# VectorE copies that free a PSUM bank get the rank of score tiles, with new planner settings

## The chip, the cores and the metric

The kernel runs on one core of a Trainium2 chip. The core has five engines with a queue of instructions each: TensorE (PE), ScalarE (ACT), VectorE (DVE), GpSimd (POOL) and SyncE (SP, which here only issues DMAs). Matmuls write into PSUM, which has eight banks of 512 fp32 values on each of 128 partitions. The metric is the time of one execution on the device, in microseconds; lower is better. The time before is the median of three runs.

## The reference

The input x has 2048 rows of 512 features. Two layers of attention and gated FFN are applied, each with a residual and a layer norm ahead:

```python
x = x + A(layernorm(x), wqkv, wo)                 # 32 heads of width 16, softmax over all 2048 keys
x = x + B(layernorm(x), w_gate, w_up, w_down)     # (gelu(x @ w_gate) * (x @ w_up)) @ w_down, width 1792
x = x + A(layernorm(x), wqkv, wo)                 # the same weights again
x = x + B(layernorm(x), w_gate, w_up, w_down)
```

Attention without a mask means 32 heads x 2048 x 2048 scores in each layer, every one of which goes through an exponential.

## The kernel before, in words

**Units and tiles.** A unit is one block of 512 queries and four heads; there are 32 units a layer (the last eight of layer two are cut in halves of 256 queries). A unit has 64 score tiles of 128 keys x 512 queries, each of which fills one PSUM bank. TensorE computes up to four tiles at a time, one for each quarter of its rows (L1555). ScalarE takes the tiles of a "slot" together, three banks or two in turn, and writes exp of them to `PT` in bf16 (L1569).

**Tiles on VectorE.** Up to about a third of the tiles may go to VectorE instead. It takes no exponential: it adds a bias, clips at zero and converts to int16 (L1609, into `PI`), so that the bits read as fp16 are roughly a power of two. Up to four such tiles make a group. For each group, three further instructions (L1649, "half-steps" in this text: `PP` = `PI` plus a constant) make the same numbers shifted by a quarter, a half and three quarters of a power, and the sum of four products with rescaled values (`VP` and three copies `VD`) smooths the error out. TensorE multiplies all of it with the values (P·V, L1701), accumulating in bank 7. When a unit is done, VectorE copies bank 7 out (L1001, L996).

**Banks.** Banks 0 to 2 and 3 to 4 are ScalarE's two slots, bank 7 the accumulator. Banks 5 and 6 float: every other product goes through them, that is, VectorE's score tiles and all "pieces" of side work. A piece is a few matmuls into one bank: Q, K and V projections (L654, L731), output projection (L654 to L1208), gate and up (L1223), down (L1287). Behind a piece, VectorE copies the bank out (L702, L721, L752, L1208, L1242 for gate, L1266 for up, L1318 and L1309 for down), and only then is the bank free again. `evac_job` (L578) is the helper that queues this copy.

**The order is written by a planner.** The Python code simulates the engines while it emits instructions: each has a modelled cost, and `sch.ready` tells when its inputs are there in the model. The main loop (L1851) follows TensorE's time and picks, in this order: the next fill of a slot when its banks are free; a batch of P·V; a piece of side work from one of five sources; a smaller batch of P·V; or filler (`keep_clock`, L1715, matmuls of zeros[...]) when the share of streaming time in the last 3.4 us is below `DENSE`.

**The job queues.** VectorE, GpSimd and SyncE get their work through `jobs` (L472). `pump_one` (L495) looks at all queued jobs of an engine, finds the earliest that could start, and among those within 0.03 us of it takes the one of the lowest rank, then the oldest. Score copies (L1609) have rank 0, as has the copy of bank 7; half-steps and most bank-freeing copies rank 1; layer norm statistics 1 or 2. [...]

**When VectorE gets a tile.** `pick` (L1428) looks through the tiles in order for one that VectorE may take, if a floating bank is free within 0.02 us and `vector_tile` (L1406) is true: VectorE's queue, its running work, the queued jobs and 0.37 us for each half-step that waits for a buffer, must come to less than `DVE_LATE`. `fill_ready` (L1469) may hold a fill back for a floating bank, as long as ScalarE still has `WAIT_D` of work.

**Side work.** The FFN of a query block runs among the score tiles of the next. `behind` (L1815) compares its progress with a schedule (`PACE`, `LAST`), in units, and `post_tol` (L1830) says by how much a piece may overrun the moment when the next fill is due.

Of the kernel before, what the change touches and what calls it, by code (L numbers as in the profile page):

```python
# [175 lines left out]
def _emit_fast(nc, es, x_in, wqkv, wo, wg, wu, wd, out, n_rep=2):  # L176
# [13 lines left out]
    NG = 2 * NCK  # L190
# [5 lines left out]
    NU = NQB * NG  # L196
# [1 line left out]
    VW = 17  # L198
    NPH = 4
    NPART = 12 if NQB > 1 else 0  # L200
    DVE_LATE = 2.83
    WAIT_D = 0.45
    OCT = 1024.0
    LOG2E = 1.4426950408889634
    QSCALE = OCT * LOG2E * DH ** -0.5
# [27 lines left out]
    NPI = 3  # L233
    PI = sb("fPI", [128, NPI, 2048], I16)
# [33 lines left out]
    sch = _Sched()  # L268
    for e in ("pe", "act", "dve", "pool", "sp"):
        sch.add_engine(e)  # L270
    BK = [("BANK", b) for b in range(8)]
# [28 lines left out]
    SW, MM = 0.107, 0.216  # L300
# [9 lines left out]
    def change(kind):  # L310
        return SW if kind_now[0] != kind else 0.0
# [54 lines left out]
    for b in range(1, NQB):  # L366
        dma("sp", "ldx%d" % b, X[:, 2 * b:2 * b + 2, :].bitcast(BF).rearrange("p a (c d) -> p (a c) d", c=2),
            x_in[0, 512 * b:512 * b + 512, :].rearrange("(a p) c -> p a c", p=128),
            w=[("XB", 4 * b + i) for i in range(4)], kb=512)
        if b == 1 and NCK > 1:  # L370
            for name, W, lo in W3:
                dma("sp", "ld1" + name, W[:, :, 128:D], wq_src[:, :, lo + 128:lo + D],
                    w=[(name, c) for c in range(1, NCK)], kb=384)
# [5 lines left out]
           r=[("ONB",)], w=[("IDN",)])  # L379

    sch.op("pool", lambda e: e.memset(QMASK[:], 0.0), w=[("QMASK",)])  # L381
    for j in range(4):
        sch.op("pool", lambda e, j=j: e.memset(QMASK[32 * j:32 * j + 16, 0:1], QSCALE), r=[("QMASK",)], w=[("QMASK",)])
    sch.op("pool", lambda e: e.tensor_scalar(QMASK[:, 1:2], QMASK[:, 0:1], -1.0, QSCALE, op0=ALU.mult, op1=ALU.add),
           r=[("QMASK",)], w=[("QMASK",)])
# [23 lines left out]
    for i in range(len(wlist)):  # L409
        k = i - w_tail  # L410
# [61 lines left out]
    jobs = {"dve": [], "pool": [], "sp": []}  # L472
    now = [0.0]
    serial = [0]

    def job(eng, prio, ops, then=None, ported=False):

        serial[0] += 1
        jobs[eng].append((prio, serial[0], ops, then, ported or eng == "pool"))

    def dve(prio, ops, then=None, ported=False):
        job("dve", prio, ops, then, ported)

    def move(prio, grp, dst, src, r, w, then=None, kb=32):

        job("sp", prio, [(lambda: dma("sp", grp, dst, src, r=r, w=w, serial=True, kb=kb), r, w, None)], then)

    def starts_of(eng):
        out = []
        for _, _, ops, _, ported in jobs[eng]:  # L490
            s = max(sch.free[eng], sch.ready(eng, ops[0][1], ops[0][2]))
            out.append(port_at(eng, s) if ported else s)
        return out

    def pump_one(t):  # L495
        for eng in ("dve", "pool", "sp"):
            if not jobs[eng] or sch.free[eng] >= t:
                continue
            starts = starts_of(eng)
            first = min(starts)  # L500
            if first >= t:
                continue
            k = min((k for k in range(len(starts)) if starts[k] <= first + 0.03), key=lambda k: jobs[eng][k][:2])
            prio, _, ops, then, ported = jobs[eng].pop(k)
            for fn, r, w, us in ops:
                o = fn() if us is None else sch.op(eng, fn, r=r, w=w, cost=us, at=starts[k])
            if ported:
                port[eng].append((starts[k], sch.free[eng]))
            if then is not None:
                then(o)  # L510
            return True
        return False
# [65 lines left out]
    def evac_job(prio, b, ops, then=None):  # L578
        def done(o):
            give_back(b)  # L580
            if then is not None:
                then(o)
        dve(prio, ops, done)

    def xn(i, alt):
        if alt == "late":
# [801 lines left out]
    dg = {"n": 0, "items": [], "uk": None, "done": [0]}  # L1388
    pp_no = [0]
    pend = {}  # L1390
# [4 lines left out]
    seg_left = {}  # L1395
# [10 lines left out]
    def vector_tile():  # L1406

        if pace["haste"]:
            return False
        if not dg["items"] and pend.get(("PI", dg["n"] % NPI)):  # L1410
            return False
        late = max(0.0, sch.free["dve"] - now[0]) + sum(op[3] for j in jobs["dve"] for op in j[2])
        late += 0.37 * len(shifts)
        return late < DVE_LATE

    def vector_bank():
# [4 lines left out]
    vb_busy = {}  # L1421
# [6 lines left out]
    def pick(look=False):  # L1428

        cap = slot_cap()  # L1430
        want_d = not look and started_all() and behind() < LAG and vector_tile()
        bd = vector_bank() if want_d else None
        if bd is None or sch.ready("pe", w=[BK[bd]]) > now[0] + 0.02:
            want_d = False
        a, d = [], None
        spare = None
        for k, x in enumerate(cur):
            if len(a) == cap and (d is not None or not want_d or k >= 12):
                break
            t = x[3]  # L1440
            if want_d and d is None and d_tile(x) and (not dg["items"] or dg["uk"] == x[:3]):
                if all(y[3] % 4 != t % 4 for y in a):
                    d = x
                    continue
                if len(a) == cap and spare is None:
                    spare = x
            if len(a) < cap:
                a.append(x)
            elif not want_d:
                break  # L1450
        return a, d if d is not None else spare
# [17 lines left out]
    def fill_ready():  # L1469

        s = slot_no[0] % 2
        if slot_open[s]:
            return None
        if slot_no[0] < 2 and not free_banks.issuperset(slot_banks()):
            return None
        pull()
        a, _ = pick(True)
        a = [x for x in a if k_here(x)]
        if not a:
            return None  # L1480
        if pend.get(("PT", pt_of())):
            return None
        keys = []
        for x in a:
            keys += tile_keys(x)
        ready = sch.ready("pe", keys, [BK[b] for b in slot_banks()[:len(a)]])
        if started_all() and not pace["haste"] and (free_banks or vb_busy):
            free = min([sch.ready("pe", w=[BK[b]]) for b in free_banks]
                       + [max(sch.free["dve"], now[0]) + 0.75 for b in vb_busy])
            if ready < free <= sch.free["act"] - WAIT_D:  # L1490
                ready = free
        return ready
# [43 lines left out]
    def a_slot(atiles, dtile):  # L1536
        both = atiles + ([dtile] if dtile is not None else [])
        tiles_filled[0] += len(both)
        bd = vector_bank() if dtile is not None else None
# [22 lines left out]
        for x in both:  # L1562
            for k in tile_keys(x):
                if k not in keys:
# [6 lines left out]
                   r=bks, w=[("PT", p)], cost=0.062 + 0.427 * na + (1.3 if table["gelu"] else 0), lat=0.16)  # L1571
# [15 lines left out]
        if dtile is not None:  # L1587
            uk = dtile[:3]
# [12 lines left out]
            def then(o):  # L1601
# [6 lines left out]
                ripe(items, gi, done)  # L1608
            dve(0, [(lambda e: e.tensor_scalar(PI[:, gi, 512 * r:512 * (r + 1)], bank(bd), DBIAS, 0.0,  # L1609
                                               op0=ALU.add, op1=ALU.max), [BK[bd]], [("PI", gi, r)], 0.6)], then)  # L1610
        if dg["items"] and (len(dg["items"]) == 4 or seg_left[dg["uk"]] < 3 and not any(
                x[:3] == dg["uk"] and d_tile(x) for x in cur)):
            flush()

# [168 lines left out]
    def post_source():  # L1783
        while True:
            if posts:
                pace["on"], pace["n"] = True, 0
                pace["haste"] = posts_done[0] == total_posts - 1 and NQB > 1
                first = 0
                for p in posts.pop(0):
                    if p is not None:  # L1790
                        first += 1
                        if first <= 9:
                            p.tol = 1.0
                        pace["n"] += (p.cost + 0.1) / 0.71
                    yield p
                posts_done[0] += 1
                pace["haste"] = pace["on"] = False
            else:
                yield None
# [5 lines left out]

    A_END = NU + NPART * (NQB - 1.0) / NQB
    B_END = A_END + NPART / NQB * min(1.0, NG / max(1.0, NPART))
    LAST = 2 * NU - NG / 2 + 2.31
    STEP = (LAST - B_END - 1.0) / (NQB - 1)
    PACE = [(NU + 1.0, A_END - 1.2)]  # L1810
    for i in range(NQB - 1):
        a = max(PACE[-1][1] if i else B_END + 1.0, NU + NG * (i + 1) + 1.0 if NG * (i + 1) > NPART else B_END + 1.0)
        PACE.append((a, LAST if i == NQB - 2 else B_END + 1.0 + STEP * (i + 1)))
# [1 line left out]
    def behind():  # L1815

        if not pace["on"]:
            return 0.0
        units = tiles_filled[0] / (4.0 * NKT)
        at = units - NG * (posts_done[0] + 1) - 1.0  # L1820
        if NQB > 1 and n_rep > 1 and NQB - 1 <= posts_done[0] < total_posts - 2:
            a, b = PACE[posts_done[0] - NQB + 1]
            f = (units - a) / (b - a)
        elif NQB > 1 and posts_done[0] == total_posts - 2:
            f = 0.5 * (at + 0.5 * NG - 1.0) / (0.5 * NG - 1.8)
        else:
            f = at / (NG - 1.5)
        return PIECES * f - pace["n"]

    def post_tol():  # L1830
        if pace["haste"] or behind() > LAG:
            return 99.0
        return 1.58 if behind() > 0 else 0.01

    def queue_source(queue):
        while True:
# [8 lines left out]
        move(3, "ldw_s%d" % p0, WOS[p0:p0 + n, :], wo[r0:r0 + n, :], [], [("WOS", p0)], None, kb=n)  # L1845

    sources = [Source(queue_source(directs), lambda: 1.0), Source(queue_source(leads), lambda: 1.0), Source(heads(), lambda: 0.1), Source(prep_source(), lambda: 0.1), Source(post_source(), post_tol)]
    DENSE = 0.67
    log = {"idle": 0.0, "warm": 0}

    while True:  # L1851
# [27 lines left out]
            limit = max(F, sch.free["act"] - 0.44) - t  # L1879
        its = pv_ready(t)  # L1880
        byj = [sum(1 for it in its if it[1] == j) for j in range(4)]
        fit = int((limit - change("col")) / MM + 0.00)
        full = min(byj)
        rest = False
        if its:
# [4 lines left out]
        press = F is None and left() and pend.get(("PT", pt_of())) or shifts and pend.get(("PP", shifts[0][0]))  # L1890
        if press and its:
            full = max(full, 1)
        want = 1 if pend.get(("PI", dg["n"] % NPI)) and not dg["items"] else 4
        keep = next((p for p in (src.peek() for src in sources) if p is not None and p.held is not None), None)
        ready_ = keep is not None and piece_ready(keep, keep.held) <= t + 0.02 and keep.cost + change("full") <= limit + 0.1
        if not (ready_ and not press) and fit >= 1 and (full >= want or full and (rest or press)):
# [887 lines left out]
```

## Time and profile before

| | |
|---|---|
| median of three runs | 1599.12 us (1598.38 to 1603.86) |
| profiled execution, its own time | 1602.76 us |
| its span, first to last instruction | 1600.4 us |
| ScalarE busy | 1520.6 us, 95% |
| TensorE busy | 1496.0 us, 93% |
| VectorE busy | 1440.3 us, 90% |
| GpSimd busy | 179.7 us, 11% |
| mean granted TensorE clock | 0.999 |
| first exponential starts, last ends | 15.1 us, 1555.8 us |

A group's row gives the line of the kernel, the engine and operation, what it writes and reads, how often it ran, the busy time and the mean duration, and behind the last bar the idle time of that engine just before these instructions, with what ended most of it. Durations of neighbouring instructions overlap a little: a VectorE copy that shows 685 ns is followed by the next start after 0.60 us. A row of the waits gives who waited for whom, total us, how many times, and the longest. "PEld" is TensorE's loading of weights, which runs beside its matmuls; a wait there is no stall of the matmuls by itself.

### The profile page before, as it was taken

The numbers are of one execution on the slowest core, as the hardware profiler recorded it, in microseconds if no ns is written. First come the engines' busy times: TensorE is split into PE (matmuls) and PEld (weight loads), VectorE is DVE, ScalarE is ACT, GpSimd is POOL, SyncE is SP. The second block draws the span as 40 slices with busy tenths as digits, with TensorE's granted clock in tenths as the row PEclk, the third lists the DMA queues.
The fourth block names the chain that finished last, engine by engine and source line by source line (L and its number), as shares of the span: only waits on it lengthen the run. The fifth ranks groups of instructions, "written<-read, shape, count | busy, mean of one in ns | idle before, by whom it ended". The sixth has DMA issues, their size and how long they took to land.

```text
span 1600.4 us, 37958 instructions
## 1 busy us (share of the span) xinstructions
PE 1496.0 (93%) x15867; PEld 499.6 (31%) x15923; DVE 1440.3 (90%) x2483; ACT 1520.6 (95%) x1306; POOL 179.7 (11%) x218
## 2 busy tenths in 40 slices
PE   8999899999999999999999999889999999999998
PEld 3333222222222222332332223222222222444455
DVE  8999999889998899988998889999889898998894
ACT  6999999999999999999999999999999999999991
POOL 3321110002100021002410002020101000200000
PEclk9999999999999999999999999999999999999999
DMA  5200111116112241114212223332314114113145
GB/s 155 61 8 6 50 28 48 50 41 141 32 48 58 81 101 35 45 53 112 79 47 61 69 72 100 97 100 71 101 38 106 49 45 126 43 36 92 30 121 174
DMA packets 168375, 112.36 MB, mean 70 GB/s; under 512 B 55048, under 2 KB 148232, under 8 KB 168200
## 3 DMA queue, kind: packets, MB, share of 16 engines
q1 hardware_dynamic: 164504, 105.28, 24.6%
q0 software_dynamic: 2112, 4.19, 1.0%
q8 instruction: 129, 2.11, 0.6%
q10 hardware_dynamic: 1584, 0.39, 0.1%
q14 instruction: 46, 0.38, 0.1%
HBM read 81.40 MB, written 19.78 MB: 63 GB/s over the span
## 4 chain that ended last, share of the span: by engine, by line
ACT 41%; PE 35%; DVE 21%; issue 1%; DMA 0%; SPq 0%; DVEq 0%
ACT fPT L1569 39%; PE fPS L1701 10%; PE fPS L1555 9%; DVE fPI L1609 9%; PE fPS L1223 8%; DVE fPP L1649 7%; PE fPS L1287 4%; PE fPS L654 2%; ACT fHT L1515 2%; DVE fHT L1242 1%; PE fPS L1721 1%; DVE fHT L1266 1%; DVE fQ L702 1%; DVE fOS L1001 1%; PE fPS L731 1%
## 5 line engine op out<-in xcount | busy, mean ns | idle before, releaser
L1569 ACT ACTIVATE fPT<-fPS 128x1536 bf16<-128x1536 f32 x1263 | 1446.7, 1269 | 35.7 <-PE fPS L1555 30.7
L1609 DVE TENSOR_SCALAR fPI<-fPS 128x512 int16<-128x512 f32 x939 | 636.6, 685 | 58.1 <-PE fPS L1555 54.7
L1555 PE MATMUL fPS<-fQ,fKT 32*128 32x512 f16 (+1 forms) x4608 | 508.2, 359 | 56.4 <-ACT fPT L1569 30.4
L1649 DVE TENSOR_SCALAR fPP<-fPI 128x2048 int16<-128x2048 int16 (+3 forms) x777 | 491.4, 656 | 12.1 <-PE fPS L1701 8.8
L1701 PE MATMUL fPS<-fPT,fVP 128*17 128x512 bf16 (+1 forms) x3548 | 456.2, 359 | 8.0 <-DVE fOS L1001 2.5
L1701 PE MATMUL fPS<-fPP,fVD 128*17 128x512 f16 (+1 forms) x3180 | 430.9, 357 | 6.4 <-DVE fPP L1649 4.9
L1555 PEld LDWEIGHTS fPS<-fQ,fKT 32*128 32x128 f16 x4608 | 137.8, 91 | 522.0 <-ACT fPT L1569 357.3
L1701 PE MATMUL fPS<-fPI,fVP 128*17 128x512 f16 (+1 forms) x1060 | 271.7, 357 | 2.8 <-DVE fOS L996 1.1
L1223 PE MATMUL fPS<-fXNT,fWR 128*128 128x512 f16 (+1 forms) x952 | 219.2, 362 | 8.6 <-DVE fPI L1609 3.2
L1701 PEld LDWEIGHTS fPS<-fPT,fVP 128*17 128x17 f16 x3548 | 118.7, 88 | 143.0 <-issue 87.4
L1701 PEld LDWEIGHTS fPS<-fPP,fVD 128*17 128x17 f16 x3180 | 116.0, 89 | 122.3 <-issue 56.2
L957 POOL TENSOR_TENSOR fAT<-fOP,fRB 128x512 f16<-128x512 f32 (+1 forms) x35 | 43.7, 1250 | 794.4 <-DMA fRB<-rscr 794.4
L1287 PE MATMUL fPS<-fWR,fHT 128*128 128x512 bf16 x388 | 109.5, 382 | 8.3 <-issue 5.1
L1223 PEld LDWEIGHTS fPS<-fXNT,fWR 128*128 128x128 bf16 x952 | 77.1, 98 | 116.2 <-DVE fPI L1609 31.3
L1266 DVE TENSOR_TENSOR fHT<-fPS,fHT 128x512 bf16<-128x512 f32 x112 | 76.4, 689 | 31.2 <-PE fPS L1223 21.8
L1242 DVE CAST fHT<-fPS 128x512 bf16<-128x512 f32 x105 | 71.4, 687 | 17.3 <-PE fPS L1223 16.9
L1721 PE MATMUL fPS<-fONB,fZV 128*17 128x512 f16 x1044 | 85.5, 394 | 1.5 <-POOL fQMASK L381 1.5
L1701 PEld LDWEIGHTS fPS<-fPI,fVP 128*17 128x17 f16 x1060 | 69.7, 88 | 38.2 <-issue 18.7
L744 POOL TENSOR_SCALAR fVD<-fVP 128x544 f16<-128x544 f16 (+1 forms) x48 | 58.3, 1214 | 155.1 <-DVE fVP L752 152.4
L606 POOL TENSOR_SCALAR fLNS<-fMV 128x2 f32<-128x2 f32 (+1 forms) x28 | 7.9, 283 | 409.6 <-DVE fMV L597 409.3
L702 DVE TENSOR_SCALAR fQ<-fPS,fQMASK 128x512 f16<-128x512 f32 (+1 forms) x72 | 46.2, 685 | 4.7 <-PE fPS L654 4.6
L1515 ACT ACTIVATE fHT<-fHT 128x3584 bf16<-128x3584 bf16 (+1 forms) x16 | 47.3, 2996 | 1.2 <-DVE fHT L1242 1.1
(89 smaller groups left out, 617.2 us busy)
## 6 DMA issues: line engine op xcount, KB each, us to landing
fWR<-in_B_w_up_dram SPq DMA_DIRECT2D x62, 256.0 KB, 2.9
fWR<-in_B_w_down_dram SPq DMA_DIRECT2D x58, 256.0 KB, 2.8
fWR<-in_B_w_gate_dram SPq DMA_DIRECT2D x57, 256.0 KB, 4.9
oscr<-fOS SPq DMA_DIRECT2D x224, 32.0 KB, 1.7
fOP<-oscr SPq DMA_DIRECT2D x28, 256.0 KB, 2.8
fRB<-rscr SPq DMA_DIRECT2D x28, 256.0 KB
fX<-in_A_x_dram POOLq DMA_DIRECT2D x4, 1024.0 KB, 5.6
xscr<-fX SPq DMA_DIRECT2D x16, 256.0 KB, 2.5
```

Source lines behind the costliest of these rows:

```text
L702: ops.append((lambda e, p=p, slot=slot: e.tensor_scalar(Q[:, slot, q0:q0 + qn], bank(b)[:, 0:qn], QMASK[:, p:p + 1], None, op0=ALU.mult), ...
L1223: ins = e.matmul(bank(bs[0])[:, w * qn:(w + 1) * qn], lhsT=wchunk(s, (ft + w) % 2, ck), rhs=XNT[:, ck, xs], start=(ck == 0), stop=(ck == N ...
L1242: evac_job(1, b, [(lambda e: e.tensor_copy(in_ht(ft), in_bank(b)), [BK[b]], fk, 0.6)], got(("gate", layer, qb, h, ft)))
L1266: (lambda e: e.tensor_tensor(in_ht(ft), in_bank(b), in_ht(ft), op=ALU.mult), [BK[b]] + fk, fk, 0.62)], got(("up", layer, qb, h, ft))))
L1287: ins = e.matmul(bank(b)[:, 0:D], lhsT=HT[:, ft, i * 128:(i + 1) * 128], rhs=wslot(s)[:, jj * D:(jj + 1) * D], start=(ft == 0), stop=(ft = ...
L1515: sch.op("act", lambda e, lo=lo, hi=hi: e.activation(HT[:, lo:hi, q0:q0 + qn], HT[:, lo:hi, q0:q0 + qn], ACTF.Gelu_apprx_tanh), r=keys, w= ...
L1555: ins = e.matmul(bank(b)[:, b0:b0 + qn], lhsT=KT[32 * j:32 * j + 32, (x[1] % NG) // 2, kt * 128:(kt + 1) * 128], rhs=Q[32 * j:32 * j + 32, ...
L1569: o = sch.op("act", lambda e: e.activation(PT[:, at:at + na, :], PS[:, b0:b0 + na, :], ACTF.Exp, scale=1.0 / (OCT * LOG2E)), r=bks, w=[("P ...
L1609: dve(0, [(lambda e: e.tensor_scalar(PI[:, gi, 512 * r:512 * (r + 1)], bank(bd), DBIAS, 0.0, op0=ALU.add, op1=ALU.max), [BK[bd]], [("PI", ...
L1649: shifts.append((s, [(lambda e: e.tensor_scalar(PP[:, s, 0:512 * n], PI[:, gi, 0:512 * n], int(OCT) * ph // NPH, None, op0=ALU.add), [("PI ...
L1701: ins = e.matmul(PS[32 * j:32 * j + VW, ACC, 0:qn], lhsT=l, rhs=r_, start=a, stop=z, tile_position=(0, 32 * j), skip_group_check=True)
L1721: ins = e.matmul(PS[32 * j:32 * j + VW, ACC, :], lhsT=ZV[:, :], rhs=ones, start=False, stop=False, tile_position=(0, 32 * j), skip_group_c ...
```

## The change

Every copy queued with `evac_job` now gets rank 0 at most, so it is queued among the score copies, the oldest first, and ahead of half-steps and statistics that could start at the same time. Since a job can now pass an older one that touches the same data, each job carries the keys that it reads and writes, and `in_order` keeps it back while an older job in any of the three queues conflicts with it. Some fifteen settings have other values.

```diff
-    DVE_LATE = 2.83
-    WAIT_D = 0.45
+    DVE_LATE = 2.61
+    WAIT_D = 0.65
...
         serial[0] += 1
-        jobs[eng].append((prio, serial[0], ops, then, ported or eng == "pool"))
+        r = frozenset(k for o in ops for k in o[1])
+        w = frozenset(k for o in ops for k in o[2])
+        jobs[eng].append((prio, serial[0], ops, then, ported or eng == "pool", r, w))
...
+    def in_order(n, r, w):
+
+        return not any(m < n and not (w.isdisjoint(r2) and w.isdisjoint(w2) and r.isdisjoint(w2))
+                       for q in jobs.values() for _, m, _, _, _, r2, w2 in q)
+
     def starts_of(eng):
         out = []
-        for _, _, ops, _, ported in jobs[eng]:
+        for _, n, ops, _, ported, r, w in jobs[eng]:
+            if not in_order(n, r, w):
+                out.append(1e9)
+                continue
...
     def evac_job(prio, b, ops, then=None):
...
-        dve(prio, ops, done)
+        dve(min(prio, 0), ops, done)
...
         late = max(0.0, sch.free["dve"] - now[0]) + sum(op[3] for j in jobs["dve"] for op in j[2])
-        late += 0.37 * len(shifts)
+        late += 0.48 * len(shifts)
         return late < DVE_LATE
...
-        if bd is None or sch.ready("pe", w=[BK[bd]]) > now[0] + 0.02:
+        if bd is None or sch.ready("pe", w=[BK[bd]]) > now[0] + 0.13:
...
-            if len(a) == cap and (d is not None or not want_d or k >= 12):
+            if len(a) == cap and (d is not None or not want_d or k >= 16):
...
-                       + [max(sch.free["dve"], now[0]) + 0.75 for b in vb_busy])
+                       + [max(sch.free["dve"], now[0]) + 0.78 for b in vb_busy])
...
-        if dg["items"] and (len(dg["items"]) == 4 or seg_left[dg["uk"]] < 3 and not any(
+        if dg["items"] and (len(dg["items"]) == 4 or seg_left[dg["uk"]] < 4 and not any(
...
-                        if first <= 9:
+                        if first <= 6:
                             p.tol = 1.0
...
-    LAST = 2 * NU - NG / 2 + 2.31
+    LAST = 2 * NU - NG / 2 + 2.00
     STEP = (LAST - B_END - 1.0) / (NQB - 1)
-    PACE = [(NU + 1.0, A_END - 1.2)]
+    PACE = [(NU + 1.0, A_END - 1.22)]
...
-        return 1.58 if behind() > 0 else 0.01
+        return 0.45 if behind() > 0 else 0.17
...
-    DENSE = 0.67
+    DENSE = 0.7
...
-        fit = int((limit - change("col")) / MM + 0.00)
+        fit = int((limit - change("col")) / MM + 0.3)
...
-        want = 1 if pend.get(("PI", dg["n"] % NPI)) and not dg["items"] else 4
+        want = 1 if pend.get(("PI", dg["n"] % NPI)) and not dg["items"] else 3
```

More of the change, by code (lines that the diff above doesn't have):

```diff
@@ L503, in pump_one @@
             k = min((k for k in range(len(starts)) if starts[k] <= first + 0.03), key=lambda k: jobs[eng][k][:2])
-            prio, _, ops, then, ported = jobs[eng].pop(k)
+            prio, _, ops, then, ported, _, _ = jobs[eng].pop(k)
             for fn, r, w, us in ops:
```

## The prediction

> **What bounds the kernel now.** I read the busy line first, then the stretch between the first full stage and the last exponential, then the costly groups.
>
> ```profile
> PE 1496.0 (93%) x15867; PEld 499.6 (31%) x15923; DVE 1440.3 (90%) x2483; ACT 1520.6 (95%) x1306; POOL 179.7 (11%) x218
> ...
> L1569 ACT ACTIVATE fPT<-fPS 128x1536 bf16<-128x1536 f32 x1263 | 1446.7, 1269 | 35.7 <-PE fPS L1555 30.7
> L1609 DVE TENSOR_SCALAR fPI<-fPS 128x512 int16<-128x512 f32 x939 | 636.6, 685 | 58.1 <-PE fPS L1555 54.7
> ...
> L1649 DVE TENSOR_SCALAR fPP<-fPI 128x2048 int16<-128x2048 int16 (+3 forms) x777 | 491.4, 656 | 12.1 <-PE fPS L1701 8.8
> ...
> L1721 PE MATMUL fPS<-fONB,fZV 128*17 128x512 f16 x1044 | 85.5, 394 | 1.5 <-POOL fQMASK L381 1.5
> ```
>
> ```profile
> 40.00:1556.00 1516.00, 1421.28 (x15152) 457.20 (x15204) 1385.51 (x2360) 1483.84 (x1271) 164.05 (x184) 1.00 0.25 65
> ```
>
> The second fence is the table of stretches: length, then busy time of PE, PEld, DVE, ACT and POOL. Between 40 and 1556 us ScalarE is busy 1483.8 of 1516.0 us, so idle 32.2; VectorE is idle 130.5 us and TensorE 94.7 us, and TensorE also spends 85.5 us on filler that computes nothing (L1721). ScalarE is the bound. Its work there is the exponentials, 1263 for all score tiles but the 939 that VectorE turns into powers of two (L1609). The end can come sooner in two ways only: fewer tiles on ScalarE, or less of those 32 us. The 44 us behind the last exponential and the first 15 us hold no scores; I leave them unchanged.
>
> One tile moved from ScalarE to VectorE is worth this. By shape, exponentials of three banks take 1482 ns and of two 1057, so a bank is 0.425 us, and a call's overhead, by the runs in the chain (48 calls in 54.47 us, 1.135 each for 2.5 banks), 0.07; shared over 2.5 banks that is 0.45 us a tile. VectorE pays one 0.60 us copy (start to start in the timeline below) and its share of half-steps, 777/939 of about 0.57 us: 1.07 us.
>
> Where would VectorE take more? The L1609 rows by 80 us stretches:
>
> ```profile
> 640.00:720.00 80.00, 30.03 (x44) 1.00 0.18 49
> ...
> 960.00:1040.00 80.00, 39.19 (x59) 0.99 0.37 99
> ...
> 1120.00:1200.00 80.00, 30.30 (x45) 1.00 0.26 71
> ```
>
> Without FFN work it takes 57 to 60 tiles in 80 us; with it, 44 to 47. There VectorE also copies out gate and up tiles, yet is busy only some 69 to 72 of 80 us: it lacks banks, not time. Only two banks float between these copies and the score tiles of VectorE.
>
> **Part 1, the rank of the copies.** This is what the rank costs before (VectorE alone, start and length):
>
> ```profile
> 496.56 0.68 DVE L1001 COPY fOS<-fPS 128x512 f32<-128x512 f32 x1
> 497.16 0.68 DVE L1609 TENSOR_SCALAR fPI<-fPS 128x512 int16<-128x512 f32 x1
> 497.76 1.89 DVE L1649 TENSOR_SCALAR fPP<-fPI 128x2048 int16<-128x2048 int16 x3
> 499.56 1.28 DVE L1266 TENSOR_TENSOR fHT<-fPS,fHT 128x512 bf16<-128x512 f32 x2
> ```
>
> The first up tile's matmuls (L1223) start at 496.71 and end at 497.74; its copy starts at 499.56, behind three half-steps of 0.60 us that free no bank. The next up tile ends at 499.03 and waits too. Both floating banks are held, and the fills at 497.68 and 498.97 go without a VectorE tile.
>
> I matched each of the 217 gate and up copies on VectorE with its matmuls by order. The copy starts 0.75 us after its last matmul on average, 0.11 in the median. Sixty copies had half-steps in between, 91 half-steps in all; 68 score copies went between as well. With equal rank the half-steps fall behind: 91 x 0.60 = 55 us of bank time comes back. The score copies that now stand in line give theirs up for the others, one bank for another, so I count them at nothing. About 170 further bank-freeing copies (Q, K, V, output projection, down, a few transposes) at the same rate give 44 us more. Together 99 us. A score tile holds its bank some 1.6 us (matmul at 496.22, copy's end at 497.84), so there is room for 62 tiles at most. They would take 66 us of the 130.5 idle on VectorE. I take a quarter, 16 tiles: half the returned time falls where no such tile is at hand or the other bank is already free, and half of the rest is refused by the backlog gate (part 3). **16 x 0.45 = 7.2 us.** Bounds: 62 tiles, 28 us; below, 0 from this alone.
>
> What a delayed half-step holds up is the P·V work on it:
>
> ```profile
> PEld fPS L1701 <- DVE fPP L1649: 52.9, 157, 1.3
> ...
> PE fPS L1701 <- DVE fPP L1649: 7.3, 19, 1.0
> ```
>
> These are TensorE waits, 7.3 us of them real stalls. TensorE takes other work meanwhile, so I count nothing. Should they double, 7 us more of TensorE is hidden by the filler; without it, it would fall on the next fill and so on ScalarE.
>
> A rule of the Trainium skill speaks against the move: in "TensorE: Matmul & The Clock Gate", section "Architectural detail: the array is 16× 32×32, not 1× 128×128", VectorE takes its instructions strictly in order. A copy ordered ahead of a ready half-step makes it wait whenever the matmuls are later than planned. The trace agrees that such waits exist:
>
> ```profile
> DVE fHT L1266 <- PE fPS L1223: 21.8, 52, 7.0
> DVE fHT L1242 <- PE fPS L1223: 16.9, 32, 1.0
> ```
>
> That is 0.46 us a wait. If all 60 moved copies paid it, VectorE would lose 28 us, 26 tiles, 11.6 us of ScalarE. By the rows each of the 60 was ready at least one half-step before it ran, so the order written for it will mostly find it ready: I take 0.
>
> **Part 2, the order guard.** It adds no instruction. A job that touches what an earlier queued job touches waits for that, also across the POOL and SP queues: a weight or spill DMA may be issued later. POOL is busy 11% and the weights land in 2.9 us, so 0, and at worst a microsecond or two at a stage's end. No transfer is added or moved past another otherwise.
>
> **Part 3, the settings.** They pull both ways. VectorE's backlog gate drops from 2.83 to 2.61 us and each waiting half-step counts 0.48 instead of 0.37: with three waiting, 1.17 us of queue is allowed instead of 1.72. That turns tiles away; it is already in the quarter above. A bank may now be 0.13 us from free instead of 0.02, and 16 instead of 12 tiles are searched: more tiles. Groups are closed with fewer than four tiles left instead of three: short groups rise (150 of 777 half-steps are short now); 30 more at about 0.15 us are 4.5 us of VectorE, hidden in its idle time.
>
> The tolerance of FFN pieces matters more. A piece (four matmuls, 1.04 us) may overrun the next fill by 1.58 us when the FFN is behind; after, by 0.45, or 0.17 when it is not. The cost before is ScalarE's wait for scores:
>
> ```profile
> ACT fPT L1569 <- PE fPS L1555: 30.7, 75, 3.8
> ```
>
> Less the 3.8 at the start, 74 waits of 0.36 us. In about 13 us of those above 0.2 us TensorE never paused: it was on other work when the fill was due. I take **half of that, 7 us**, with bounds of 0 and 20. The price is that FFN pieces come later; they are also paced to finish earlier (2.31 to 2.00 units; a unit is 64 tiles, 24 us, so 7.5 us), which I let cancel.
>
> Filler density, 0.67 to 0.70:
>
> ```profile
> 1036.00:1042.00 6.00, 5.22 (x39) 1.26 (x39) 4.30 (x7) 4.83 (x5) 0.00 (x0) 0.72 0.49 132
> ```
>
> Here the granted clock fell to half for one window of 3.4 us; matmuls took 0.65 instead of 0.39 us and ScalarE then waited 1.17 us. The same page of the Trainium skill (section "Why this matters for your kernels") asks only that TensorE not idle for some 3 us at a time; the longest idle time in the five microseconds before was 0.96. By the rule more filler buys nothing; by the row it can save 1.2. I take 0.5, since filler also costs TensorE time. Smaller batches of P·V (3 rounds for 4) add switches on TensorE, inside the 85.5 us of filler.
>
> **Sum.** The profiled execution took 1602.8 us (span 1600.4 and 2.4 around it). 1602.8 - 7.2 - 7 - 0.5 = 1588.1. It lies 3.7 above the median of the runs, 1599.1; scaled, 1599.1 x 1588.1/1602.8 = 1584.4. I say **1585**.
>
> **Rivals.**
> *No change you can measure.* The gate, not the bank, sets how many tiles VectorE takes: in stretches without FFN it is full already, and half-steps that wait longer keep the gate shut. Tiles stay at 939, only some idle time goes: 1602.8 - 4, about 1595 on the runs' scale (1592 to 1603). For it: 131 us of idle VectorE beside an open gate would be odd. Against: L1609 itself waits 54.7 us for scores, so VectorE does run dry. This is also the case in which the change does not do what it says.
> *Slower.* Where the gate bites in the full stretches (78 of 80 us busy), 0.55 us less queue lets VectorE run dry there. Each 1% of its 1516 us is 14 tiles, 6.4 us. It decides from about 18 tiles lost (921 copies, +8 us); I price it at 24 lost, +11: **1610**. Against: the bank tolerance opens what the gate shuts.
> *Much faster.* VectorE fills a third of its idle time: 40 tiles, 18 us, and 10 of ScalarE's idle go: 1602.8 - 28, **1571**. For it: the 99 us of bank time would allow it.
>
> **How the numbers follow.** Two measurements of this kernel can be told apart at about 0.5%, 8 us. Forecast 0.60 (its own range 1577 to 1591), no change 0.24, slower 0.08, much faster 0.08. Faster by over 0.5%, below 1591: 0.60 + 0.08 = 0.68; within, 0.24; slower, 0.08. The range 1573 to 1602 leaves out the slow case, the top of the middle one and the far end of the fast one, under 2 in 10.
>
> **What would show it.** Part 1: the gate and up copies start within about 0.4 us of their matmuls on average, and no half-step runs between; L1609 counts near 955, up in the FFN stretches; exponentials near 1257. Part 3: ScalarE's wait for scores near 23 us. I am wrong if L1609 counts fall while the copies do come sooner (the gate), if L1649's releases of L1701 double and ScalarE's idle time with them, or if the time behind the last exponential grows beyond 45 us because FFN work has slipped.

## The result

The changed kernel takes 1592.85 us (median, 1591.99 to 1593.35), against 1600.97 us for the kernel before, measured beside it. The ratio is 0.9948, with a 95% interval of 0.9927 to 0.9969. That is 8.1 us, 0.5%: faster, as forecast, inside the stated range, and a little over half of the 14.1 us that the forecast named (1599.1 to 1585). It is just outside the forecast's own range (1577 to 1591) and inside that of the rival "no change" (1592 to 1603).

The rows of the changed kernel's page that answer to those of before (its lines are 10 further down: L1579 is the exponential, L1619 VectorE's score copy, L1659 the half-step, L1731 the filler):

```profile
PE 1518.2 (95%) x16150; PEld 504.7 (32%) x16150; DVE 1431.8 (90%) x2485; ACT 1519.0 (96%) x1308; POOL 177.4 (11%) x218
...
L1579 ACT ACTIVATE fPT<-fPS 128x1536 bf16<-128x1536 f32 x1265 | 1445.0, 1280 | 24.6 <-PE fPS L1565 19.9
L1619 DVE TENSOR_SCALAR fPI<-fPS 128x512 int16<-128x512 f32 x935 | 633.5, 685 | 58.5 <-PE fPS L1565 53.3
...
L1659 DVE TENSOR_SCALAR fPP<-fPI 128x2048 int16<-128x2048 int16 (+3 forms) x783 | 492.6, 648 | 12.3 <-PE fPS L1711 9.0
...
L1731 PE MATMUL fPS<-fONB,fZV 128*17 128x512 f16 x1292 | 105.7, 391 | 1.5 <-POOL fQMASK L381 1.5
```

VectorE did not take more tiles: 935 instead of 939, so ScalarE has two calls more. What fell is the idle time ahead of the exponentials, 35.7 to 24.6 us. TensorE has more filler, 1292 matmuls for 1044.

The waits of the changed kernel (who for whom, total us, times, longest):

```profile
DVE fHT L1276 <- PE fPS L1233: 22.5, 52, 7.2
ACT fPT L1579 <- PE fPS L1565: 19.9, 49, 3.5
DVE fHT L1252 <- PE fPS L1233: 8.8, 19, 1.0
...
PE fPS L1711 <- DVE fPP L1659: 4.5, 13, 1.1
```

ScalarE waits for scores 49 times instead of 75. VectorE's waits for gate and up tiles went down, from 38.7 to 31.3 us, and TensorE's stalls for half-steps from 7.3 to 4.5.

The rank works as written. VectorE's own timeline around an up tile, and the tile's matmuls on TensorE:

```profile
705.61 0.68 DVE L1619 TENSOR_SCALAR fPI<-fPS 128x512 int16<-128x512 f32 x1
706.21 0.68 DVE L1276 TENSOR_TENSOR fHT<-fPS,fHT 128x512 bf16<-128x512 f32 x1
706.81 1.28 DVE L1659 TENSOR_SCALAR fPP<-fPI 128x2048 int16<-128x2048 int16 x2
```

```profile
705.13 1.04 PE L1233 MATMUL fPS<-fXNT,fWR 128*128 128x512 f16 x4
```

The matmuls end at 706.17, the copy starts at 706.21, and two half-steps now run behind it. Over all 217 gate and up copies the mean time from matmul to copy fell from 0.75 to 0.34 us, and the half-steps in between from 91 to 13.

### The profile page after: what moved, and what is told of

The parts are those of the page before. It is cut to its first block, busy times and chain, and to the rows that moved or that the text cites. A ratio compares the mean times of both kernels' runs of the same rounds, so it can differ in the third digit from the quotient of the medians.

```text
span 1589.9 us, 38476 instructions
## 1 busy us (share of the span) xinstructions
PE 1518.2 (95%) x16150; PEld 504.7 (32%) x16150; DVE 1431.8 (90%) x2485; ACT 1519.0 (96%) x1308; POOL 177.4 (11%) x218
## 4 chain that ended last, share of the span: by engine, by line
PE 43%; ACT 43%; DVE 12%; issue 1%; DMA 0%; SPq 0%; DVEq 0%
ACT fPT L1579 40%; PE fPS L1711 13%; PE fPS L1565 12%; PE fPS L1233 10%; DVE fPI L1619 5%; PE fPS L1297 5%; DVE fPP L1659 5%; PE fPS L664 2%; ACT fHT L1525 2%; PE fPS L741 1%; PE fPS L1731 1%; ACT L1525 1%; DVE fHT L1252 0%; DVE fQ L712 0%; DVE fHT L1276 0%
## 5 line engine op out<-in xcount | busy, mean ns | idle before, releaser
L1579 ACT ACTIVATE fPT<-fPS 128x1536 bf16<-128x1536 f32 x1265 | 1445.0, 1280 | 24.6 <-PE fPS L1565 19.9
L1619 DVE TENSOR_SCALAR fPI<-fPS 128x512 int16<-128x512 f32 x935 | 633.5, 685 | 58.5 <-PE fPS L1565 53.3
L1565 PE MATMUL fPS<-fQ,fKT 32*128 32x512 f16 (+1 forms) x4608 | 504.1, 359 | 44.3 <-ACT fPT L1579 31.5
L1659 DVE TENSOR_SCALAR fPP<-fPI 128x2048 int16<-128x2048 int16 (+3 forms) x783 | 492.6, 648 | 12.3 <-PE fPS L1711 9.0
L1711 PE MATMUL fPS<-fPP,fVD 128*17 128x512 f16 (+1 forms) x3159 | 441.9, 357 | 5.4 <-DVE fPP L1659 4.2
L1711 PE MATMUL fPS<-fPI,fVP 128*17 128x512 f16 (+1 forms) x1053 | 267.8, 358 | 1.6 <-DVE fOS L1006 0.7
L1711 PEld LDWEIGHTS fPS<-fPP,fVD 128*17 128x17 f16 x3159 | 120.3, 89 | 115.3 <-issue 47.4
L1297 PE MATMUL fPS<-fWR,fHT 128*128 128x512 bf16 x428 | 118.3, 383 | 0.4 <-DMA fWR<-in_B_w_down_dram 0.3
L1731 PE MATMUL fPS<-fONB,fZV 128*17 128x512 f16 x1292 | 105.7, 391 | 1.5 <-POOL fQMASK L381 1.5
L1276 DVE TENSOR_TENSOR fHT<-fPS,fHT 128x512 bf16<-128x512 f32 x112 | 76.5, 689 | 32.8 <-PE fPS L1233 22.5
L1711 PEld LDWEIGHTS fPS<-fPI,fVP 128*17 128x17 f16 x1053 | 69.4, 88 | 38.7 <-issue 16.4
```

What stands on the lines that cost most here:

```text
L1276: (lambda e: e.tensor_tensor(in_ht(ft), in_bank(b), in_ht(ft), op=ALU.mult), [BK[b]] + fk, fk, 0.62)], got(("up", layer, qb, h, ft))))
L1297: ins = e.matmul(bank(b)[:, 0:D], lhsT=HT[:, ft, i * 128:(i + 1) * 128], rhs=wslot(s)[:, jj * D:(jj + 1) * D], start=(ft == 0), stop=(ft = ...
L1565: ins = e.matmul(bank(b)[:, b0:b0 + qn], lhsT=KT[32 * j:32 * j + 32, (x[1] % NG) // 2, kt * 128:(kt + 1) * 128], rhs=Q[32 * j:32 * j + 32, ...
L1579: o = sch.op("act", lambda e: e.activation(PT[:, at:at + na, :], PS[:, b0:b0 + na, :], ACTF.Exp, scale=1.0 / (OCT * LOG2E)), r=bks, w=[("P ...
L1659: shifts.append((s, [(lambda e: e.tensor_scalar(PP[:, s, 0:512 * n], PI[:, gi, 0:512 * n], int(OCT) * ph // NPH, None, op0=ALU.add), [("PI ...
L1711: ins = e.matmul(PS[32 * j:32 * j + VW, ACC, 0:qn], lhsT=l, rhs=r_, start=a, stop=z, tile_position=(0, 32 * j), skip_group_check=True)
```

## How ScalarE's time is counted here

ScalarE sets the end, so each kernel's span is split along it. **Head**: until the first exponential. **Exponentials**: each at its closest spacing, start to start, 1.331 us for three banks and 0.904 for two. **Rest**: all other time until the last exponential or gelu (gelu, table loads, and waiting). **Tail**: from there to the end. The 3.1 to 3.4 us around the computing instructions are left out everywhere. The starts and ends are those of the profiled executions.

| kernel | tiles on VectorE | mean lag of gate/up copies | head | exponentials | rest | tail | late starts | measured, ratio to before (95%) |
|---|---|---|---|---|---|---|---|---|
| before | 939 | 0.75 | 15.1 | 1411.2 | 135.4 | 35.5 | 61.7 | about 1600 |
| the change | 935 | 0.34 | 14.6 | 1413.0 | 127.2 | 31.7 | 47.2 | 1592.9, 0.9948 (0.9927 to 0.9969) |
| rank alone | 958 | 0.34 | 16.6 | 1402.7 | 144.4 | 31.6 | 70.9 | 1598.6, 0.9987 (0.9974 to 1.0000) |
| settings alone | 919 | 0.67 | 14.5 | 1420.1 | 134.0 | 32.8 | 60.8 | 1606.4, 1.0033 (1.0023 to 1.0044) |
| tolerance alone | 930 | 0.70 | 15.0 | 1415.2 | 138.7 | 32.7 | 58.7 | 1605.3, 1.0027 (1.0015 to 1.0039) |
| rank and tolerance | 954 | 0.31 | 14.8 | 1404.5 | 132.1 | 31.8 | 58.2 | 1587.9, 0.9914 (0.9885 to 0.9944) |
| the same, bank limit 0.03 | 958 | 0.32 | 15.0 | 1402.7 | 131.1 | 31.5 | 57.8 | 1587.1, 0.9917 (0.9901 to 0.9934) |
| change, old gate | 946 | 0.34 | 16.4 | 1408.0 | 138.5 | 32.1 | 59.0 | 1600.0, 0.9995 (0.9983 to 1.0007) |
| change, WAIT_D 0.46 | 951 | 0.38 | 14.7 | 1405.8 | 135.6 | 34.4 | 63.0 | 1596.2, 0.9968 (0.9956 to 0.9979) |
| change, old tolerance | 947 | 0.38 | 16.6 | 1407.6 | 140.6 | 33.8 | 56.3 | 1604.0, 1.0017 (1.0006 to 1.0027) |
| rank, tolerance, nine first | 958 | 0.39 | 16.3 | 1402.7 | 142.0 | 34.4 | 69.8 | 1599.7, 0.9993 (0.9985 to 1.0002) |
| rank, six first | 959 | 0.34 | 16.7 | 1402.2 | 141.8 | 31.8 | 68.2 | 1597.4, 0.9974 (0.9962 to 0.9987) |
| change, bank limit 0.12 | 926 | 0.36 | 14.5 | 1417.0 | 124.2 | 33.2 | 50.3 | 1594.4, 0.9953 (0.9936 to 0.9971) |

"Late starts" sums, over pairs of neighbouring exponentials, what the spacing has beyond the closest one (single terms under 0.02 us and over 3 us left out). It is larger than the idle time that the page gives, since neighbouring exponentials overlap. In the two longest groups by shape of the kernel "rank and tolerance":

```profile
L1579 ACT ACTIVATE fPT<-fPS 128x1536 bf16<-128x1536 f32 x628 | 932.6, 1485 | 29.0 <-PE fPS L1565 24.3
L1579 ACT ACTIVATE fPT<-fPS 128x1024 bf16<-128x1024 f32 x629 | 667.2, 1061 | 3.5 <-PE fPS L1565 2.3
```

1485 ns against a spacing of 1331, 1061 against 904: an exponential that starts up to 0.15 us late leaves no idle time at all in the rows. So before the change the page shows 30.7 us of waiting where the spacing shows 61.7.

I also sorted the late starts by what TensorE was doing before the fill that came late. Before: 20.2 us behind gate or up matmuls, 19.4 behind a stall of TensorE on VectorE (a bank or a half-step), 22.1 behind all the rest. After: 15.0, 12.4 and 19.8. This sorting is made from the order of starts, one cause for each late start, so it is a guide and not a measurement of causes; for the stalls of TensorE its own rows of waits, further down, say more.

## The experiments

**Theories.** *Banks*: the sooner copies give VectorE more tiles and free TensorE from stalls. *Settings*: the gain is that FFN pieces overrun the fills less. *Gate*: the new settings turn away the tiles that the rank would have brought.

### Rank alone, settings alone

Rank alone: all settings as in the kernel before, with the changed queue. (With the guard but the old rank, the planner writes the same instructions in the same order as before.)

```diff
-        dve(prio, ops, done)
+        dve(min(prio, 0), ops, done)
```

> The kernel before with the new rank and the order guard alone, all settings as before. Late starts of exponentials (start-to-start beyond 1.33 us for three banks and 0.90 for two) sum to 61.7 us before and 47.2 after the whole change. Bank theory (the copies that come sooner free TensorE, and with it ScalarE): the part behind stalls of TensorE on VectorE falls from 19.4 to about 12 us, time about 7 us below before, and with the old, wider backlog gate the score copies rise above 939. Settings theory (the gain is the smaller overrun of FFN pieces): the sum stays near 60 us and the time within 3 us of before. Gate and up copies start about 0.35 us behind their matmuls under both.

```profile
L1579 ACT ACTIVATE fPT<-fPS 128x1536 bf16<-128x1536 f32 x1255 | 1439.1, 1270 | 43.4 <-PE fPS L1565 38.6
L1619 DVE TENSOR_SCALAR fPI<-fPS 128x512 int16<-128x512 f32 x958 | 646.3, 683 | 53.1 <-PE fPS L1565 49.9
```

1598.6 us, ratio 0.9987. The sooner banks do bring tiles, 19 of them, and 8.5 us of exponentials go. But ScalarE's waiting rises, 30.7 to 38.6 us in the rows and 61.7 to 70.9 in the spacing; of the latter, the part behind gate and up matmuls goes from 20.2 to 25.8 us. The stalls on VectorE stay (19.4 to 20.2). So the bank theory is right on the tiles and wrong on the stalls. In time this is no clear difference from before: the interval reaches 1.0000. My reading is that a free bank also lets an FFN piece start, and with a tolerance of 1.58 us it starts when the next fill is nearly due; the tolerance runs below test that, and bear it out only in part.

Settings alone: the change with the old rank.

```diff
-        dve(min(prio, 0), ops, done)
+        dve(prio, ops, done)
```

> The changed kernel with the old rank for the bank-freeing copies; all new settings stay. Settings theory: late starts near 50 us, the part behind FFN matmuls near 15 us, time near the changed kernel's, 8 us below before. Bank theory: the copies are late again (0.75 us behind their matmuls), late starts near 60 us, time near before. With the narrower gate and late copies the score copies on VectorE fall below 935, and each tile less costs 0.45 us: at 915 about 10 us of slowdown against the changed kernel.

```profile
L1579 ACT ACTIVATE fPT<-fPS 128x1536 bf16<-128x1536 f32 x1271 | 1456.2, 1278 | 34.0 <-PE fPS L1565 28.9
L1619 DVE TENSOR_SCALAR fPI<-fPS 128x512 int16<-128x512 f32 x919 | 622.4, 684 | 62.0 <-PE fPS L1565 57.5
```

1606.4 us, 1.0033: slower. 20 tiles are lost, 8.9 us more exponentials, and the late starts are those of before. The settings are no gain of their own; they are settings for a queue in which the copies come soon.

### Rank and tolerance, a square

```diff
-                        if first <= 9:
+                        if first <= 6:
...
-        return 1.58 if behind() > 0 else 0.01
+        return 0.45 if behind() > 0 else 0.17
```

on the kernel before, with the new rank:

> The kernel before with the new rank, the order guard and, of the settings, only the tolerance of pieces (0.45 and 0.17, six first pieces). If the rank and the tolerance each bring their half and the other settings nothing: late starts near 47 us, score copies near 939 or above because the gate is the wide one, and a time at or below the changed kernel's, 1585 to 1593. If the other settings are needed to keep the gain: near 1600.

and without it:

> The kernel before with the new tolerance of pieces alone (0.45 and 0.17, six first pieces); the old rank. With the three measured ones (before 939 tiles and late starts of 61.7 us; rank alone 958 and 70.9; both 954 and 58.2) this fills the square. If rank and tolerance need each other: copies late by 0.7 us, score copies below 939, late starts 55 to 62 us, time 1600 to 1607, so that the two alone sum to about nothing and together give 12 us. If the tolerance alone pays: late starts near 52 us and a time 6 us or more below before.

Both together take 1587.9 us, 0.9914; the tolerance alone 1605.3, 1.0027. Against the kernel before, timed with each, the rank alone gave -1 us, the tolerance alone +5, both -12 (by the ratios -2, +4 and -14). Here are the rows with both:

```profile
L1579 ACT ACTIVATE fPT<-fPS 128x1536 bf16<-128x1536 f32 x1257 | 1439.5, 1273 | 32.5 <-PE fPS L1565 26.7
L1619 DVE TENSOR_SCALAR fPI<-fPS 128x512 int16<-128x512 f32 x954 | 644.7, 684 | 49.6 <-PE fPS L1565 44.8
```

Beside rank alone, the tiles stay (954 for 958), ScalarE's wait for scores falls from 38.6 to 26.7 us, and the rest on ScalarE from 144.4 to 132.1. A further 1.8 us of the gap in time lie in the head and go with a clock window told of below. Without the rank, the small tolerance costs tiles (930) and leaves the rest at 138.7. In these orders the two need each other.

Taken apart once more, with the rank in both:

> The kernel before with the new rank, the guard and the tolerance of 0.45 and 0.17, but nine first pieces with a tolerance of 1 us as before, not six. If the tolerance for most pieces is what counts: within 4 us of 1588, late starts near 58 us. If the three pieces at each FFN's start (layer norm and transposes mostly) matter as much: near 1598, as with the rank alone.

> The kernel before with the new rank, the guard and six first pieces instead of nine, and the old tolerance of 1.58 and 0.01. If the tolerance for most pieces is what counts: near rank alone, 1598, late starts near 70 us. If the first pieces do it: near 1588.

1599.7 and 1597.4 us. Neither half of the tolerance edit keeps the gain: tiles are at 958 and 959, but the rest is at 142 in both. (Six first alone keeps a small part: 0.9974, 0.9962 to 0.9987.) That the general tolerance alone does it is refuted, and with it a part of my reading above. Only with the first six pieces (not nine) and the small tolerance together does the rest come down by some 10 us. The seventh to ninth pieces are gate tiles (four output projections come first), not layer norm and transposes as I had written, so both edits bear on the same kind of piece. But there are nine FFN runs at most, so "nine first" changes the limit of no more than 27 pieces. Why half of the edit gives nothing is left open, and chance of the order is not excluded: neither half was run with a neighbour, as the whole edit was (below).

### Where the tiles went: gate and WAIT_D

```diff
-    DVE_LATE = 2.61
+    DVE_LATE = 2.83
...
-        late += 0.48 * len(shifts)
+        late += 0.37 * len(shifts)
```

> The changed kernel with the old backlog gate (2.83 us, 0.37 us for each waiting half-step). Gate theory (the narrower gate ate the tiles that the sooner banks would have allowed): score copies rise from 935 to 945 or more, ScalarE's exponentials fall by 0.4 for each, and the time falls by 0.45 us for each, some 5 us. Rival (a deeper VectorE queue makes banks and P.V late again): copies rise but late starts rise with them and the time is the same or longer.

```diff
-    WAIT_D = 0.65
+    WAIT_D = 0.46
```

> The changed kernel with WAIT_D at 0.46 us in place of 0.65, almost the old 0.45: a fill is held for a floating bank with less work left on ScalarE. If this setting, with the gate, ate the tiles that the rank brought: score copies 950 or more in place of 935. If a tile is then worth its 0.45 us, 1585 to 1589; if fills held longer make ScalarE late, late starts rise from 47 to 55 us or more and the time stays near 1593.

The score copies of the old gate and of the smaller WAIT_D:

```profile
L1619 DVE TENSOR_SCALAR fPI<-fPS 128x512 int16<-128x512 f32 x946 | 639.3, 684 | 60.2 <-PE fPS L1565 56.1
```

```profile
L1619 DVE TENSOR_SCALAR fPI<-fPS 128x512 int16<-128x512 f32 x951 | 642.1, 683 | 53.3 <-PE fPS L1565 48.9
```

Each brings tiles back, 11 and 16, and neither makes the kernel faster: 1600.0 us with the old gate and 1596.2 with WAIT_D, for 1592.9. The first is clearly slower (0.9995 against 0.9948, intervals apart); for WAIT_D the intervals overlap. The exponentials fall by 5.0 and 7.2 us as they should at 0.45 a tile. The rest on ScalarE rises by 11.3 and 8.4. So the gate theory is right about where the tiles went and wrong about their worth: among these settings a tile costs at least what it saves (1.8 us of the old gate's loss are in the head, with the clock window told of below).

With WAIT_D the place is to be seen, in the rows of TensorE's waits. The largest row of score fills that wait for VectorE, in the kernel before, in the change, and in the change with WAIT_D at 0.46:

```profile
PE fPS L1555 <- DVE fPI L1609: 11.0, 25, 0.9
```

```profile
PE fPS L1565 <- DVE fPI L1619: 4.7, 10, 1.0
```

```profile
PE fPS L1565 <- DVE fPI L1619: 7.7, 18, 0.9
```

Over all rows in which a fill waits for VectorE it is 20.1, 6.0 and 14.4 us. Rank alone has 15.7, settings alone 6.9. In all five kernels with 0.65 the sum is 6.0 to 8.2 us, in all eight with 0.45 or 0.46 it is 11.8 to 20.1. So fewer stalls of the fills, which the bank theory put down to the rank, belong to WAIT_D: a fill is held for a floating bank less often.

### The tolerance in the changed kernel

The reverse of the tolerance edit above, on the changed kernel:

> The changed kernel with the old tolerance of pieces (1.58 and 0.01, nine first pieces). If the tolerance is what keeps the sooner banks from being spent on overruns: late starts go from 47 back to 60 us or more, most of it behind FFN matmuls, and the time to 1600 to 1606, near rank alone. If the other settings do it: late starts below 52 us, time within 3 us of 1593.

```profile
ACT fPT L1579 <- PE fPS L1565: 39.0, 72, 7.5
```

1604.0 us, 1.0017. The wait for scores doubles from 19.9 us to 39.0, and all of the gain goes, though 12 tiles come back. The time is as expected; the sum of late starts, 56.3, is below the 60 expected, since one wait of 7.5 us is above its limit of 3. That one wait (7.45 us, up to 808.3 us, where TensorE is still at K and V projections of the second layer) is 7.5 of the 19.1 us that the row rises by. It is no overrun of a single piece: no other kernel here waits more than 2.8 us at a stretch between 760 and 840 us. The other 11.6 us are spread over the kernel.

### How much is the luck of one order

> The kernel before with the new rank, the guard and the new tolerance, as in the run that took 1587.9, and with the bank limit at 0.03 instead of 0.02 us: a change too small to mean anything in itself, but the whole order of instructions after the first difference is another one. It shows how much of a difference between two orders is chance. If the gain belongs to rank and tolerance: 955 tiles within 5, late starts within 4 us of 58, time 1585 to 1592. If the order was a lucky one: 1593 or more.

> The changed kernel with the bank limit at 0.12 instead of 0.13 us, a change that means nothing in itself but gives another order. If 1593 is what these settings give: within 3 us of it. If the order that was chosen is a lucky one among its neighbours: 1596 or more.

1587.1 against 1587.9 us, and 1594.4 against 1592.9: a small step in one limit reshuffles the order and, in these two pairs, moves the time by 1 or 2 us. The difference of 5 to 7 us between the two families stands in both pairs; one of 2 us between two kernels in the table should not be read. Two pairs are few, so the true spread may be larger. In the second pair, 9 tiles fewer (926) cost 4.0 us of exponentials and the rest fell by 3.0, the same exchange again.

## Why the prediction was right, and where it was off

The direction was right and the range wide enough, but half of the working did not come true. The forecast was 16 more tiles and 7 us less waiting; there were 4 tiles fewer and the waiting fell by more than that (10.8 us in the rows). In both signs, and in its time of about 1595, that is the rival "no change". A sign that I had named for being wrong came too, though small: the L1609 counts fell while the copies came sooner. The number was held up in part by luck: 3.8 us of the tail, on which I had counted nothing, and a full clock, worth more than the 0.5 us counted for it.

**The sum.** Between the two profiled executions the parts are: head -0.5, exponentials +1.8, rest -8.2, tail -3.8, together -10.7 of a span that fell by 10.5. The forecast had -7.2 on exponentials, -7 on waiting and -0.5 for the clock, -14.7. (A slip in it: 170 copies at the rate of 55 us for 217 are 43 us of bank time, not 44; the 16 tiles stay.)

- **Copies come sooner: right.** Lag 0.34 us where about 0.4 was named, 13 half-steps in between where 91 were; the forecast named none.
- **16 tiles, 7.2 us: the term that failed.** The rank on its own brings 19 tiles and takes 8.5 us off the exponentials, near the size named. But I wrote that the narrower gate was already in the quarter, which without the gate would have been a half, 31 tiles; so the rank brings fewer than I thought, and the settings take more. As a whole they cost 23 tiles beside the rank alone (958 to 935), and 1.8 us more of exponentials were measured where 7.2 fewer were forecast. The gate put back returns 11 and WAIT_D 16, and I had given WAIT_D no term at all.
- **7 us of waiting: right in kind, a little small.** The wait row fell by 10.8 us, the rest by 8.2. The tolerance is at work in it, as the old one doubles the wait, but not alone: with the old gate the row is 28.6 us and with WAIT_D at 0.46 it is 31.2, for 19.9. The number of first pieces had no term either. What I did not see is that less waiting is also needed to keep the first term, as rank alone raises the waits by as much as it saves.
- **The bound of 0 for "this alone" was not the lower end.** Rank alone has 9 us more of the rest: a cost of the rank that I had not priced. I had counted the score copies in line at nothing and looked for harm at the half-steps; by the sorting of late starts it lay with the pieces (20.2 to 25.8 us behind gate and up matmuls).
- **Half-steps that come later: right.** TensorE's stalls for them did not double; 7.3 us went to 4.5, and to 7.5 with rank alone.
- **VectorE's strict order: right to take 0.** VectorE's waits for gate and up tiles fell by 7.4 us, and by 6.1 with rank alone (38.7 to 32.6). Mostly the matmuls had ended when a copy's turn came; no run here tests the rule itself.
- **The clock: too small, its cause open.** All four executions of the change and all seven of its neighbour had a full granted clock (1.000); of 122 executions of the kernel before, 23 did. Those 23 have a median of 1599.0 us, all 122 one of 1600.2, the four beside the change one of 1601.0, so an estimate for the clock is 1 to 2 us of the 8.1. But "settings alone", with the same density, has a window at 1037 us, and the change with the old gate two there. So the density does not by itself prevent it.
- **The rivals.** "No change" had the outcome: tiles stayed at 939 within 4, idle time went, and its 1595 is nearer to 1592.9 than 1585 is. Against it, the gain is clear of the noise (0.9927 to 0.9969). Its reason, half-steps that keep the gate shut, is not needed for that: with the rank and the old gate the tiles rise at once.
- **The time behind the last exponential** was said to stay, and more than 45 us was a sign of being wrong; it went from 44.6 to 47.1. The last gelus lie in it: in the change ScalarE waits 5.2 us before the last of them, which my split counts under "rest". From the last gelu to the end it fell from 35.5 to 31.7. In the other kernels that is 31.5 to 34.4, with the old rank too, so it is not the rank's. Split at the last exponential, the rest ahead of it fell by 14.3 us and the time behind it rose by 2.5. The cause stays open.

## A version that beats both

The kernel before with the rank, the guard and the tolerance edit, and no other setting changed, takes 1587.9 us (0.9914 of before, 0.9885 to 0.9944); with the bank limit at 0.03 us, 1587.1 (0.9917, 0.9901 to 0.9934). That is about 5 us below the full change in the medians. The two were not timed side by side, and the intervals of their ratios overlap; those of their two neighbours just do not. Two of the eight executions took 1594 us, longer than any of the change; both had a granted clock of 0.995. It keeps the tiles (954 and 958) and a part of the shorter waits (58 us of late starts, for 61.7 before and 47.2 after the full change).

## What to carry to other kernels

A resource that comes free sooner can be spent by a taker you do not mean. Before giving it priority, find every taker; here the rank paid only when side work with leave to overrun was held back at the same time. Price both sides of an exchange from the bounding engine, its own work and its waiting; a setting that moves tiles off it is worth nothing when the waiting rises by as much. When an order of instructions is planned, run a meaningless neighbour of each candidate, and read only differences that are larger than theirs. Look at the granted clock of each execution before you compare two kernels.

## What the runs showed of the hardware

Windows of half clock come and go, between kernels and between executions of one kernel. In five of the kernels here (rank alone, the old gate, the old tolerance, nine first, six first) a window at 8 to 9 us ran at half clock, and their first exponential starts at 16.3 to 16.7 us instead of 14.5 to 15.1. The stretch from 6 to 14 us of rank alone, and of before (the column behind POOL's time is the granted clock):

```profile
6.00:14.00 8.00, 5.96 (x63) 2.41 (x52) 5.97 (x16) 1.19 (x2) 1.47 (x3) 0.79 1.09 343
```

```profile
6.00:14.00 8.00, 6.59 (x76) 2.90 (x69) 7.34 (x20) 1.20 (x2) 1.92 (x5) 1.00 1.09 340
```

0.79 is one window of 3.4 us at half speed in 8. It goes with about 1.6 us more of head. In all five, TensorE had just stood idle for 1.8 to 2.2 us at a stretch (from 6.1 to 6.5 us on); in the eight others the longest idle time at that place is 0.5 to 1.4 us. Later in the kernels no such line can be drawn: in the five microseconds ahead of the window at 1038 us of the kernel before no idle time was above 0.96 us, while rank alone is idle for 1.56 us at 790 us and keeps its full clock.

The granted clock is also on record for every execution. Of 122 of the kernel before, the 23 at 1.000 have a median of 1599.0 us, the 58 at 0.999 one of 1600.1, the 22 at 0.998 one of 1600.9, and the seven at 0.995 or below took 1604.8 to 1611.3: about 1.1 us for each 0.001. The kernel "rank and tolerance" took 1583.7 us at 1.000 and 1594.0 and 1594.3 at 0.995. So a good part of the spread of one kernel goes with its clock.
